# A fused mLSTM attention, token mixer and gated MLP on one core: hand-placed memory, recorded and planned operations, 384-token blocks, no 64-row matmuls

## The chip, the cores and the metric

The kernel runs on one core of one Trainium2 chip. The number is the device time of one execution in microseconds (us); lower is better. TensorE is PE in the profile (its weight loads PEld), VectorE is DVE, ScalarE is ACT, GpSimd is POOL; SP issues the DMAs.

## The reference

Batch 2, 8 heads, 768 tokens, head width 40, model width 320. Three stages follow each other:

```
attention, per batch and head, over tokens t:
  m_new = max(f + m, i);  C = exp(f + m - m_new) C + exp(i - m_new) v k^T;  n likewise with k
  y = sigmoid(o) * (C q) / max(|n q|, 1)
mixer:  u = x + (relu(x^T w_tok1) w_tok2)^T;   x = u + relu(u w_ch1) w_ch2      (256 and 1536 wide)
gMLP:   h = gelu(x w_in); u, v = halves of h (512 each); v = layernorm(v) * g
        x + (u * (w_sg v + b)) w_out
```

The weights come as float64 words, except w_sg.

## The kernel before

**Attention** works in 12 chunks of 128 tokens (6 for each batch). For a chunk, p1 (L322) makes the decay matrix: a matmul psM, 8 exponents on ACT (L336, one for each head, with the row's gate as a bias), a mask on POOL (L338). p2 (L342) makes the scores psS (L350) in full float32 and multiplies them into E on DVE (L351). p3 (L353) makes the chunk's own part psO (L393), the part that comes from the chunks before, psI (L387), which DVE scales (L389) and adds (L396), the new state (psC, L367; DVE L378), the denominators (L400 to L403) and the output `nat` (L406). A float32 matmul shows as two records of the trace.

**Everything behind it** uses a split: each operand is a high part in float32r and a low part, and a product is three matmuls (high by high, low by high, high by low). A weight piece is loaded as float64 words, turned into float32 by one ACT and four DVE instructions (L192 to L198), then split (L170, L171). There are 26 such pieces. The token mixer is tok1 (L430) and tok2 (L473). The channel mixer, ch_phase (L490), runs over blocks of 256 tokens: ch1 makes 128 hidden rows of a block, relu_split (L441) splits them on ACT and DVE, ch2 adds them into two accumulators of 320 columns. The gMLP is part_v (512 columns), and part_u with u, sgu and outp, again over 256 tokens.

Model width 320 is 128 + 128 + 64. For the last 64 rows the high part of the activations stands in partitions 0 to 63 and the low part in 64 to 127 of one tile, so one matmul over 128 rows (L501) makes two of the products, and a second one over the first 64 rows (L502) makes the third. The same pair stands in part_v (L612) and u (L644). These are the 64-row matmuls: 72 + 12 + 24 = 108 in all.

**Order.** Tiles come from pools, and a scheduler orders the instructions by a priority that the author sets by hand in microseconds (`pri(t)`, the tables T_..). Attention of the second batch is interleaved with the channel mixer of the first. Each engine then runs its own list in that order, and waits at an instruction until its inputs are there. All loads are issued by SP in one list.

Of the kernel before, what the change touches and what calls it, by code (L numbers as in the profile page):

```python
# [42 lines left out]
T_AM = [8.0, 13.27, 18.55, 23.82, 29.09, 34.37, 63.39, 71.06, 78.74, 86.41, 94.09, 101.76]
T_AS = [10.69, 13.27, 18.55, 23.82, 27.97, 34.37, 83.43, 71.06, 78.74, 86.41, 92.01, 99.68]
T_AO = [15.0, 17.58, 22.85, 23.54, 27.86, 36.77, 71.33, 79.0, 86.68, 94.35, 99.95, 107.63]
T_AL = [0.5, 0.92, 8.93, 14.2, 19.47, 24.75, 49.62, 57.29, 64.97, 69.12, 74.09, 81.76]
T_T1 = [48.97, 57.14, 64.51, 65.65, 73.01, 80.38, 135.94, 136.48, 137.03, 137.58, 138.13, 138.68]
T_LD = [0.83, 4.35, 7.88, 7.36, 14.94, 18.46, 47.02, 53.09, 59.15, 65.22, 65.06, 71.13, 66.11, 72.67, 79.23, 85.79, 92.35, 167.65, 170.15, 169.68, 174.08, 155.26, 203.02, 224.33, 211.55, 214.86, 196.5, 224.48, 228.45, 251.69, 254.57, 257.07]
T_CV = [8.5, 10.56, 15.55, 19.08, 22.61, 26.13, 55.44, 61.51, 67.58, 67.42, 73.84, 79.56, 82.84, 89.4, 95.96, 102.52, 109.08, 156.7, 165.74, 170.17, 170.47, 181.94, 225.1, 226.29, 227.53, 218.73, 222.99, 224.86, 229.21, 254.43, 278.38, 257.45]
B_CL = [0, 0, 0, 0, 0, 0, 0, 0, 0, 0, 0, 0, 0, 0, 0, 0, 0, 0, 0, 0, 0, 0, 0, 0, 0, 0]  # L50
B_LO = [0, 0, 1, 1, 1, 1, 1, 1, 1, 1, 0, 0, 0, 1, 1, 1, 1, 1, 0, 1, 0, 0, 0, 1, 1, 0, 1, 1, 1, 1, 1, 1]
B_X = [1, 0]
B_V = [1, 1]
B_G = [1, 0]
I32 = mybir.dt.int32
I64 = mybir.dt.int64
# [5 lines left out]

def asf(t):
    return t.bitcast(F32)


@with_exitstack
def tile_mlstm_mixer_gmlp(
# [20 lines left out]
    mm = nc.tensor.matmul  # L89

    def pri(t):
        tc.cur_priority = int(t * 1000)

# [1 line left out]
    base = ctx.enter_context(tc.tile_pool(name="base", bufs=1))  # L95
    ps_m = ctx.enter_context(tc.tile_pool(name="ps_m", bufs=2, space=PSUM))
    ps_acc = ctx.enter_context(tc.tile_pool(name="ps_acc", bufs=2, space=PSUM))

    con = base.tile([128, 131], F32, name="con")
    ident = con[:, 0:128]  # L100
    bdm = con[0:120, 128:131]
    nat = [base.tile([128, NC, DM], F32, name=f"nat{b}") for b in range(B)]
    wst = ctx.enter_context(tc.tile_pool(name="wst", bufs=2))

    def new_uT(pool):
        return [(pool.tile([128, 3, 256], F32R, tag=f"uThi{i}", name=f"uThi{i}"),
                 pool.tile([128, 2, 256], F32R, tag=f"uTlo{i}", name=f"uTlo{i}")) for i in range(3)]

    m1 = ctx.enter_context(tc.tile_pool(name="m1", bufs=1))
    at_cm = tc.tile_pool(name="at", bufs=2, side="right")  # L110
    at = at_cm.__enter__()
    ps_a_cm = tc.tile_pool(name="ps_a", bufs=4, space=PSUM, side="right")
    ps_a = ps_a_cm.__enter__()

# [1 line left out]
    gt_cm = tc.tile_pool(name="gt", bufs=1, side="right")  # L116
    gt = gt_cm.__enter__()
    gates_in = gt.tile([128, 284], F32, name="gates_in")
    fg, ig = gates_in[:, 0:128], gates_in[:, 128:256]
    hm, ind6, ind12 = gates_in[:, 256:264], gates_in[:, 264:270], gates_in[:, 270:282]  # L120
    neg, cap = gates_in[:, 282:283], gates_in[:, 283:284]
    selg = gt.tile([128, 360], F32, name="selg")
    nc.sync.dma_start(out=gates_in, in_=gates_d)
    nc.sync.dma_start(out=con, in_=con_d)

    qT_t, kT_t, kvo_t = {}, {}, {}
    NSET, N3 = 3, 6
    kTm = [at.tile([120, 3, 3, 128], F32, name=f"kTm{i}", bufs=1) if i < 2 else
           m1.tile([120, 3, 3, 128], F32, tag="c2_3", name="kTm2") for i in range(NSET)]
    for t in kTm:  # L130
        nc.gpsimd.memset(t, 0.0)

    def load_chunk(n):
        b, c = divmod(n, NC)
        i = n % NSET if n < N3 else n % 2
        own = i < 2
        qt = (at if own else m1).tile([120, 3, 128], F32, tag=f"qT{i}" if own else "c2_4", name="qT", bufs=1)
        nc.sync.dma_start(out=qt, in_=qT_d[b, c])
        kt = kTm[i]
# [8 lines left out]
    def eng(flag):  # L148
        return nc.gpsimd if flag else nc.vector

    def load_f32(i, pool, tag, src):
        """The float32 values of piece i of the weights; float64 words pass through slot `tag` of `pool`."""
        n = src.shape[1] // (2 if src.dtype == I32 else 1)
        t = wst.tile([128, 768], F32, tag="wt", name="wt", bufs=3)[:, :n]
        pri(T_LD[i])
        if src.dtype == I32:
            raw = pool.tile([128, n, 2], I32, tag=tag, name=f"r_{tag}", bufs=1)
            nc.sync.dma_start(out=raw.rearrange("p n w -> p (n w)"), in_=src)
            pri(T_CV[i])
            to_f32(raw, t, eng(B_CL[i]))  # L160
        else:
            nc.sync.dma_start(out=t, in_=src)
            pri(T_CV[i])
        return t

    def split_piece(i, pool, tag, src):
        """Tile [128, 2, n] in slot `tag` of `pool`: the float32r high parts, then the low parts, of src."""
        t = load_f32(i, pool, tag, src)
        w = pool.tile([128, 2, t.shape[1]], F32R, tag=tag, name=f"w_{tag}", bufs=1)
        nc.scalar.copy(w[:, 0, :], t)  # L170
        eng(B_LO[i]).tensor_tensor(out=w[:, 1, :], in0=t, in1=asf(w[:, 0, :]), op=ALU.subtract)  # L171
        return w
# [28 lines left out]
    def i32(src, a, b):  # L201
        return src[:, a:b].bitcast(I32)
# [491 lines left out]
    for _ in part_v(0):  # L694
        pass
# [110 lines left out]
```

## Time and profile before

| | |
|---|---|
| median of 3 executions | 430.89 us (430.25 to 435.47) |
| the profiled execution: its span, and the only time given of it | 430.5 us |
| PE busy (pipelined matmuls, modelled ends) | 408.4 us, 95% |
| DVE / ACT / POOL busy | 283.7 / 178.4 / 122.8 us |
| matmul records, all instructions | 2629, 7027 |
| bytes moved | 31.14 MB |

Busy time of PE is not work at its peak: a record of a matmul lasts longer than the distance to the next one's start. How long a matmul keeps TensorE is read from the distance of two starts in the timeline. The granted clock stands beside each stretch: 1.00 is the upper of two levels (2.4 GHz), 0.50 the lower (1.2 GHz).

### The profile page before, as it was taken

How to read it: one execution, taken by the hardware profiler on the slowest of the kernel's cores; microseconds unless marked ns; L12 is line 12 of the kernel's file. 1: busy time of each engine (PE TensorE's matmuls, PEld its weight loads, DVE VectorE, ACT ScalarE, POOL GpSimd, SP SyncE). 2: the span in 40 equal slices, each digit the busy share in tenths (PEclk: the TensorE clock that was granted, in tenths of full speed). 3: DMA queues.
4: the chain of work that ended last, by engine and by line, in shares of the span. 5: the costliest groups of instructions: out<-in, count | busy, mean ns of one | idle time of the engine just before them, and what ended most of it. 6: DMA issues, size and time to landing. Idle time of an engine off the chain costs nothing.

```text
span 430.5 us, 7027 instructions
## 1 busy us (share of the span) xinstructions
PE 408.4 (95%) x2629; PEld 365.5 (85%) x2629; DVE 283.7 (66%) x600; ACT 178.4 (41%) x464; POOL 122.8 (29%) x135
## 2 busy tenths in 40 slices
PE   4798898869999999999999999999999999999996
PEld 4697897858899998999888887788878899999996
DVE  5879867997997982279882257445567755455544
ACT  1757455675555521154541153332544522222321
POOL 5537537461223330010110052312626431200000
PEclk9999597996999999999999999999999999999999
DMA  7945354342521000062212030000000000000000
GB/s 225 303 166 205 122 191 158 122 170 87 197 66 49 2 27 12 0 209 63 97 43 69 0 112 0 2 0 2 1 2 2 2 32 0 32 30 17 17 32 32
DMA packets 12239, 31.14 MB, mean 72 GB/s; under 512 B 1644, under 2 KB 6444, under 8 KB 12204
## 3 DMA queue, kind: packets, MB, share of 16 engines
q1 hardware_dynamic: 12204, 30.68, 21.5%
q8 instruction: 21, 0.34, 0.3%
q14 instruction: 14, 0.11, 0.1%
HBM read 28.71 MB, written 1.97 MB: 71 GB/s over the span
## 4 chain that ended last, share of the span: by engine, by line
PE 85%; DVE 8%; issue 2%; ACT 2%; POOL 2%; DMA 1%; POOLq 0%; DVEq 0%; ACTq 0%
PE acc L516 7%; PE ps L502 5%; PE acc L518 5%; PE pss L655 5%; PE acc L517 5%; PE psO L393 4%; PE ps L498 4%; PE pss L657 4%; PE ps L499 4%; PE pss L656 4%; PE ps L500 4%; PE psS L350 3%; PE psu L644 2%; PE psC L367 2%; PE ps L501 2%
## 5 line engine op out<-in xcount | busy, mean ns | idle before, releaser
L442 ACT ACTIVATE a<-ps 128x256 fp32r<-128x256 f32 x72 | 27.8, 386 | 85.4 <-PE ps L502 85.4
L443 DVE SCALAR_TENSOR_TENSOR a<-ps,a 128x256 fp32r<-128x256 f32 x72 | 30.3, 421 | 45.5 <-ACT a L442 45.3
L516 PE MATMUL acc<-w_c,a 128*128 128x320 f32 x144 | 50.8, 354 | 0.2 <-ACT a L442 0.2
L517 PE MATMUL acc<-w_c,a 128*128 128x320 f32 x144 | 44.4, 309 | 0.0
L518 PE MATMUL acc<-w_c,a 128*128 128x320 f32 x144 | 44.3, 310 | 0.0
L498 PE MATMUL ps<-uThi,w_c 128*128 128x256 f32 x144 | 42.6, 296 | 0.0
L655 PE MATMUL pss<-w_c,v 128*128 128x256 f32 x144 | 42.2, 293 | 0.0
L499 PE MATMUL ps<-uTlo,w_c 128*128 128x256 f32 x144 | 41.4, 287 | 0.0
L500 PE MATMUL ps<-uThi,w_c 128*128 128x256 f32 x144 | 41.2, 286 | 0.0
L657 PE MATMUL pss<-w_c,v 128*128 128x256 f32 x144 | 40.5, 281 | 0.0
L656 PE MATMUL pss<-w_c,v 128*128 128x256 f32 x144 | 40.3, 280 | 0.0
L350 PE MATMUL psS<-qT,kTm 120*128 120x128 f32 (+1 forms) x192 | 31.4, 318 | 3.4 <-DVE E L351 2.5
L580 ACT ACTIVATE sq<-psu 128x256 f32<-128x256 f32 x24 | 9.2, 384 | 59.7 <-PE psu L644 59.7
L516 PEld LDWEIGHTS acc<-w_c,a 128*128 128x128 f32 x144 | 26.9, 187 | 8.0 <-issue 0.7
L171 POOL TENSOR_TENSOR w_c<-wt,w_c 128x768 fp32r<-128x768 f32 (+1 forms) x13 | 22.9, 1775 | 35.4 <-ACT w_c L170 35.3
L350 PEld LDWEIGHTS psS<-qT,kTm 120*128 120x128 f32 (+1 forms) x192 | 28.7, 226 | 4.2 <-DVE E L351 2.7
L336 ACT ACTIVATE E<-psM,wT 128x128 f32<-128x128 f32 x96 | 27.5, 380 | 8.7 <-PE psM L332 8.3
L393 PEld LDWEIGHTS psO<-kvo,E 128*128 128x128 f32 x192 | 28.9, 224 | 0.6
L655 PEld LDWEIGHTS pss<-w_c,v 128*128 128x128 f32 x144 | 27.3, 190 | 2.2
L498 PEld LDWEIGHTS ps<-uThi,w_c 128*128 128x128 f32 x144 | 28.0, 194 | 1.0 <-issue 0.7
L338 POOL TENSOR_SCALAR_AFFINE_SELECT E<-E 128x512 f32<-128x512 f32 x24 | 18.5, 772 | 34.1 <-ACT E L336 34.1
L393 PE MATMUL psO<-kvo,E 128*128 128x41 f32 x192 | 28.2, 302 | 0.0
(196 smaller groups left out, 1115.1 us busy)
## 6 DMA issues: line engine op xcount, KB each, us to landing
kvo<-in_kvo_dram SPq DMA_DIRECT2D x12, 504.0 KB
r_c<-in_ch_dram SPq DMA_DIRECT2D x5, 768.0 KB
r_c<-in_ch_dram SPq DMA_DIRECT2D x6, 640.0 KB
wt<-in_wsg_dram SPq DMA_DIRECT2D x6, 384.0 KB
qT<-in_qT_dram SPq DMA_DIRECT2D x12, 180.0 KB
kTm<-in_kT_dram SPq DMA_DIRECT2D x36, 60.0 KB
out_dram<-y SPq DMA_DIRECT2D x12, 160.0 KB
r_wA<-in_tok_dram SPq DMA_DIRECT2D x3, 512.0 KB
```

What stands on the lines that cost most here:

```text
L350: mm(ps[:, j, :], kt[0:r, jj, g, :], qt[0:r, g, :], start=True, stop=True)
L393: mm(psO[:, h, :], E[h // 4][:, h % 4, :], v1[:, h, :], start=True, stop=True)
L443: nc.vector.scalar_tensor_tensor(out=lo, in0=ps, scalar=0.0, in1=asf(hi), op0=ALU.max, op1=ALU.subtract)
L498: mm(ps, c1(0, k, m), hi[:, k, :], start=(k == 0), stop=False)
L499: mm(ps, c1(0, k, m), lo[:, k, :], start=False, stop=False)
L500: mm(ps, c1(1, k, m), hi[:, k, :], start=False, stop=False)
L516: mm(acc[j], ah[:, js], wh, start=(m == m0), stop=False)
L517: mm(acc[j], ah[:, js], wl, start=False, stop=False)
L518: mm(acc[j], al[:, js], wh, start=False, stop=(m == m2 - 1))
L655: mm(ps, v[:, 0, ds_], wsg[s][:, 0, ts], start=(s == 0), stop=False)
L656: mm(ps, v[:, 0, ds_], wsg[s][:, 1, ts], start=False, stop=False)
L657: mm(ps, v[:, 1, ds_], wsg[s][:, 0, ts], start=False, stop=(s == NC - 1))
```

## The change

The whole kernel is recorded and then ordered by a planner; memory is placed by hand. What differs in the computation:

- **No 64-row matmuls.** `transpose_split` copies the last 64 columns twice side by side, so that the transposed tile has the same 64 rows in both halves; the weights' tile has the high part above the low part. Two matmuls over 128 rows (L688, L689) then make all products. Same for v (L815, L816) and u (L841, L842).
- **Blocks of 384 tokens** instead of 256 in ch1, u and sgu. ch2 and the output matmuls keep 320 columns and have three accumulators.
- **Exponents in one pass.** The row's gate is put into the matmul's left operand (LR), so one ACT instruction of 512 columns makes four heads. LR is filled through four small DMAs of gate rows (L441) and ACT copies (L444).
- **Queries scaled.** A small matmul psW (L554, three for a chunk) spreads the decay of the queries; DVE multiplies it into q (L555). Then the part from earlier chunks and the chunk's own part add up in the same PSUM tile (L581, L583), and L389, L396 and the copy L398 fall away.
- Old and new state: ACT scales the old one (L567), DVE or POOL adds (L575). Sigmoid as 1 + tanh, the factor 2 in the denominator.
- **Order.** Every operation is recorded with its tiles' regions. PE keeps the order of the program, but may take a later matmul when the next one's inputs are late by the planner's durations; the other engines go by when the matmul that needs them is due. Low parts of splits go to DVE or POOL as the planner finds them free. In the program the attention of both batches stands ahead of the channel mixer of either: chunk n's p3 stands beside p1 of chunk n + 2, p2 of n + 1, tok1 of n - 1 and, from n = 7, tok2 of the first batch.

The diff, cut:

```diff
-            mm(ps, c1(0, 2, m), hi[:, 2, :], start=False, stop=False)
-            mm(ps, c1(1, 2, m), hi[0:64, 2, :], start=False, stop=True)
+                mm(p, w[:, ms], hi[:, 2, ts], start=False, stop=False)
+                mm(p, w[:, ms], lo[:, 2, ts], start=False, stop=True)
...
-        nc.scalar.copy(hi[:, 0:2, sl], ps[:, 0:2, :])
-        nc.scalar.copy(hi[0:64, 2, sl], ps[0:64, 2, :])
+        tl = tl_s[s % 2]
+        act.copy(tl.rearrange("p (r n) -> p r n", r=2), nat[:, b, s, 256:320].unsqueeze(1).to_broadcast([128, 2, 64]))
+        pe.transpose(p[:, 2, :], tl, ident)
+        act.copy(hi, p)
+        dve.tensor_tensor(out=lo, in0=p, in1=asf(hi), op=ALU.subtract)
...
+    def split_tails(name, col, n, src):
+        t = to_f32(name, col, n, src)
+        a, b = sb(name, col, n, F32R), sb(name, col + n, n, F32R)
+        act.copy(a[lo], t[lo])
+        flex.tensor_tensor(out=a[up], in0=t[lo], in1=asf(a[lo]), op=ALU.subtract)
...
-        NB = 256
+NB = 384
...
-                for j in range(4):
-                    h = 4 * hf + j
-                    nc.scalar.activation(out=E[:, j, :], in_=ps[:, j, :], func=AF.Exp,
-                                         bias=wTv[b][:, 2, h, c:c + 1])
+            mm(p, LR[:, n, :], MR[b][:, 4 * hf:4 * hf + 4, :], start=True, stop=True)
+            act.activation(out=E[:, hf], in_=p.rearrange("p (j t) -> p j t", j=4), func=AF.Exp)
...
-                nc.vector.tensor_tensor(out=t1, in0=psI, op=ALU.mult,
-                                        in1=wTv[b][:, 0, :, c].unsqueeze(2).to_broadcast([128, H, 41]))
+            act.activation(out=qm, in_=asf(wq_t[b]), func=AF.Copy, scale=ind6[:, c:c + 1])
+            for g in range(3):
+                mm(psW[:, g, :], selr[:, 120 * g:120 * g + 120], qm, start=True, stop=True)
+            dve.tensor_tensor(out=qs, in0=psW, in1=qt, op=ALU.mult)
...
+        act.activation(out=dn[:, 1, :], in_=psO[:, :, 40], func=AF.Abs)
+        dve.tensor_scalar(out=dn[:, 0, :], in0=dn[:, 1, :], scalar1=1.0, scalar2=2.0, op0=ALU.max, op1=ALU.mult)
...
+        for o in reversed(ops):
+            tail = 0.0 if o.eng == "PE" else 2.4 + o.nbytes / 3.0e5 if o.eng == "SP" else o.dur
+            for s in o.suc:
+                d = s.due - s.dur - (0.0 if same else o.lat + self.LAT)
+                o.due = min(o.due, d)
+            o.key = o.i if o.eng == "PE" else o.due - tail
...
+    for n in range(N):
+        if n + 2 < N:
+            p1(n + 2)
+        if n + 1 < N:
+            p2(n + 1)
+        p3(n)
+        if n + 3 < N:
+            load_chunk(n + 3)
+        for i in early.get(n, ()):
+            tok_weights(i)
+        for f in late.get(n, ()):
+            f()
+        b, c = divmod(n, NC)
+        if n >= 1:
+            m = n - 1
+            tok1(m // NC, m % NC)
+        if n == NC:
+            tok_hidden()
+        if n > NC:
+            s = n - NC - 1
+            tok2(0, s, X)
+            transpose_split(0, s, X)
...
+    ch_steps(jobs, extra)
+    Z, Q = (2, 3, 4), (0, 1)
+    for i, (b, blk, d) in enumerate(seq):
+        part_sgu(b, blk, d, Q)
...
+    with tc.manual_schedule():
+        plan.issue()
```

What this makes of the engines' lists is shown at three places. First PE in the channel mixer, one step of ch1 (ps) and the ch2 matmuls behind it. Before:

```order
L498 MATMUL ps_2379<-uThi_2102,w_c_00_1084 128x256
L499 MATMUL ps_2379<-uTlo_2103,w_c_00_1084 128x256
L500 MATMUL ps_2379<-uThi_2102,w_c_00_1084 128x256
L498 MATMUL ps_2379<-uThi_2102,w_c_01_1095 128x256
L499 MATMUL ps_2379<-uTlo_2103,w_c_01_1095 128x256
L500 MATMUL ps_2379<-uThi_2102,w_c_01_1095 128x256
L501 MATMUL ps_2379<-uThi_2102,w_c_02_1106 128x256
L502 MATMUL ps_2379<-uThi_2102,w_c_02_1106 128x256
L516 MATMUL acc<-w_c_1_1133,a 128x320
```

And now the same step, with L684 to L689 for L498 to L502 and L699 to L701 for L516 to L518:

```order
L684 MATMUL ps<-uT,c__149 128x384
L685 MATMUL ps<-uT,c__149 128x384
L686 MATMUL ps<-uT,c__149 128x384
L684 MATMUL ps<-uT,c__151 128x384
L685 MATMUL ps<-uT,c__151 128x384
L686 MATMUL ps<-uT,c__151 128x384
L688 MATMUL ps<-uT,c__153 128x384
L689 MATMUL ps<-uT,c__153 128x384
L699 MATMUL ps<-c__156,a 128x320
```

A step has the same eight ch1 matmuls, 384 columns wide, with no 64-row one among them (L502 was it); behind it stand nine ch2 matmuls instead of six, and there are 48 steps instead of 72.

Second PE in the attention of the second batch in the changed kernel, from one chunk's p1 (L528) over p2 (L540), transposes of the first batch (L645, L648), psW (L554), the new state (L563) to psO (L581, L583):

```order
L528 MATMUL ps<-MR,LR 128x512
L540 MATMUL ps<-qT,kTm 128x128 x3
L645 MATMUL ps<-con,nat 128x128 x2
L648 MATMUL ps<-con,tail 128x128
L540 MATMUL ps<-qT,kTm 128x128 x2
L528 MATMUL ps<-MR,LR 128x512
L540 MATMUL ps<-qT,kTm 128x128 x3
L554 MATMUL ps<-qm,selr 120x128 x3
L563 MATMUL ps<-wv,kvo 120x123 x2
L563 MATMUL ps<-wv,kvo 120x82
L630 MATMUL ps<-x,w__137 128x320
L581 MATMUL ps<-nb,qs 128x123 x2
```

Where the kernel before had matmuls of ch1 and ch2 between those of the second batch's chunks, only tok1, tok2 and transposes stand there now; the first ch1 matmul comes behind the last chunk's psO.

Third DVE at the end of the attention in the changed kernel, from the last chunk's output (L588) to the first split weights of ch2 (`c__156`); `rc` and `wt` are weight pieces on their way to float32:

```order
L588 TENSOR_TENSOR nat<-tn,dn 128x320
L368 SCALAR_TENSOR_TENSOR wt<-rc__152,wt 128x768
L652 TENSOR_TENSOR uT<-ps,uT 128x3x128
L387 TENSOR_TENSOR c__153<-wt,c__153 64x768
L652 TENSOR_TENSOR uT<-ps,uT 128x3x128
L636 SCALAR_TENSOR_TENSOR hl<-ps,hh 128x320 x2
L775 TENSOR_SCALAR gln<-gln 128x4
L363 TENSOR_SCALAR wt<-wt 128x640
L364 TENSOR_SCALAR wt<-wt 128x640
L366 SCALAR_TENSOR_TENSOR wt<-rc__155,wt 128x640
L639 TENSOR_TENSOR nat<-ps,nat 128x320
L368 SCALAR_TENSOR_TENSOR wt<-rc__155,wt 128x640
```

The conversion of the first ch2 piece starts only behind the last chunk's output; two relu splits and the piece's low part (L377) follow, and the first ch2 matmul (L699) waits for that.

## Rows read from the trace of the kernel before

**Rows 1.** The page, part 1 and 2: PE's busy time; its clock by slice.

```profile
PE 408.4 (95%) x2629; PEld 365.5 (85%) x2629; DVE 283.7 (66%) x600; ACT 178.4 (41%) x464; POOL 122.8 (29%) x135
...
PEclk9999597996999999999999999999999999999999
```

**Rows 2.** Windows: length, then busy us (instructions) by engine, clock, DMA.

```profile
core 0: us, PE busy (x) PEld busy (x) DVE busy (x) ACT busy (x) POOL busy (x), PEclk, DMA share, GB/s
0.00:104.00 104.00, 85.49 (x497) 78.95 (x498) 82.34 (x156) 56.56 (x162) 54.91 (x58) 0.87 0.52 173
42.00:56.00 14.00, 12.17 (x54) 11.60 (x55) 11.48 (x24) 5.59 (x20) 7.27 (x9) 0.51 0.39 128
104.00:431.00 327.00, 322.88 (x2134) 286.51 (x2132) 201.36 (x445) 121.82 (x304) 67.84 (x77) 1.00 0.12 40
```

**Rows 3.** Timeline of PE: start, duration, line; around a 64-row matmul (L502).

```profile
179.56 0.28 PE L500 MATMUL ps<-uThi,w_c 128*128 128x256 f32 x1
179.68 0.28 PE L501 MATMUL ps<-uThi,w_c 128*128 128x256 f32 x1
179.88 0.38 PE L502 MATMUL ps<-uThi,w_c 64*128 64x256 f32 x1
180.19 0.41 PE L437 MATMUL acc<-x,w_wA 128*128 128x320 f32 x1
180.44 0.31 PE L438 MATMUL acc<-x,w_wA 128*128 128x320 f32 x1
...
180.88 0.31 PE L438 MATMUL acc<-x,w_wA 128*128 128x320 f32 x1
```

**Rows 4.** Groups by line and shape: 64-row matmuls (count, busy, mean).

```profile
L502 PE MATMUL ps<-uThi,w_c 64*128 64x256 f32 x72 | 27.7, 385 | 0.0
...
L644 PE MATMUL psu<-xT,w_wB 64*128 64x256 f32 x12 | 4.6, 381 | 0.0
...
L612 PE MATMUL psv<-w_wA,xT 64*128 64x512 f32 x6 | 3.0, 499 | 0.0
```

**Rows 5.** Timeline of PE: float32 matmuls early, and at full clock.

```profile
24.23 1.77 PE L393 MATMUL psO<-kvo,E 128*128 128x41 f32 x8
...
59.45 0.83 PE L350 MATMUL psS<-qT,kTm 120*128 120x128 f32 x6
60.12 0.98 PE L393 MATMUL psO<-kvo,E 128*128 128x41 f32 x8
60.93 0.36 PE L350 MATMUL psS<-qT,kTm 80*128 80x128 f32 x1
```

**Rows 6.** Groups by line, DVE's and ACT's: count, busy us, mean ns.

```profile
L351 DVE TENSOR_TENSOR E<-psS,E 128x512 f32<-128x512 f32 x24 | 16.4, 683 | 7.6 <-PE psS L350 6.3 <-POOL E L338 1.2
L194 DVE TENSOR_SCALAR wt<-wt 128x512 int32<-128x512 int32 (+3 forms) x26 | 15.8, 610 | 0.1
L193 DVE TENSOR_SCALAR wt<-wt 128x512 f32<-128x512 f32 (+3 forms) x26 | 13.9, 537 | 0.5 <-ACT wt L192 0.4
L378 DVE SCALAR_TENSOR_TENSOR cb<-cb,decT,ct 120x123 f32<-120x123 f32 (+1 forms) x24 | 11.1, 501 | 2.2 <-ACT ct L373 2.0
L196 DVE SCALAR_TENSOR_TENSOR wt<-r_c,wt 128x640 int32<-128x640 int32 (+1 forms) x11 | 10.1, 916 | 0.0
L406 DVE TENSOR_TENSOR nat<-th,dn 128x320 f32<-128x320 f32 x12 | 7.9, 657 | 0.8 <-POOL th L405 0.7
L402 DVE TENSOR_SCALAR dn<-dn 128x8 f32<-128x8 f32 x12 | 5.1, 425 | 0.0
L396 DVE TENSOR_TENSOR t<-psO,t 128x328 f32<-128x328 f32 x10 | 4.9, 491 | 2.9 <-PE psO L393 2.9
...
L336 ACT ACTIVATE E<-psM,wT 128x128 f32<-128x128 f32 x96 | 27.5, 380 | 8.7 <-PE psM L332 8.3
```

**Rows 7.** The line of the chunks' outputs: durations, first and last start.

```profile
L406 DVE TENSOR_TENSOR nat<-th,dn x12: 475/489/1018, 29.6 to 158.2; 128x320 f32<-128x320 f32 x12
```

**Rows 8.** Timeline of PE: the last matmul.

```profile
426.83 0.31 PE L676 MATMUL pso<-w_x,gs 128*128 128x320 f32 x1
```

More of the change, by code (lines that the diff above doesn't have):

```diff
@@ L103, in tile_mlstm_mixer_gmlp @@
[L103 to L113, printed above, removed]
@@ L127, in tile_mlstm_mixer_gmlp @@
-    NSET, N3 = 3, 6
-    kTm = [at.tile([120, 3, 3, 128], F32, name=f"kTm{i}", bufs=1) if i < 2 else
-           m1.tile([120, 3, 3, 128], F32, tag="c2_3", name="kTm2") for i in range(NSET)]
-    for t in kTm:
-        nc.gpsimd.memset(t, 0.0)
+    plan = Plan(nc)
+    for d in (qT_d, kT_d, kvo_d, gates_d, con_d, selg_d, tok1_d, tok2_d, ch1_d, ch2_d, win_d, wsg_d, wout_d,
+              gln_d, bsg_d, out):
+        plan.dram.add(d.tensor.name)
+    pe, act, dve, pool, sp = (Engine(plan, e) for e in ("PE", "ACT", "DVE", "POOL", "SP"))
@@ L133, in load_chunk @@
+    qs_s = [r_tmp.take("qs", 384)[0:120].rearrange("p (g t) -> p g t", g=3) for _ in range(2)]
+    qm_s = [r_x.take("qm", 128, F32R) for _ in range(2)]
+    th_s = [r_tmp.take("th", 320).rearrange("p (h d) -> p h d", h=H) for _ in range(2)]
+    tn = r_tmp.take("tn", 320).rearrange("p (h d) -> p h d", h=H)
+    dn_s = [r_x.take("dn", 16).rearrange("p (r h) -> p r h", r=2) for _ in range(2)]
     def load_chunk(n):
         b, c = divmod(n, NC)
-        i = n % NSET if n < N3 else n % 2
-        own = i < 2
@@ new lines, in tile_mlstm_mixer_gmlp, with tok_hidden, tok2 @@
+    hh, hl = (sb(nm, WK + 6144 + 640 * i, 640, F32R).rearrange("p (m n) -> p m n", m=2)
+              for i, nm in enumerate(("hh", "hl")))
+    def tok_hidden():
+        for m in range(2):
+            relu_split(ps[:, ACC[m], 0:DM], hh[:, m, :], hl[:, m, :])
+    def tok2(b, s, banks):
+        p = bank(banks)[:, 0:DM]
+        for k in range(2):
+            mm(p, w2(0, k, s), hh[:, k, :], start=(k == 0), stop=False)
+            mm(p, w2(1, k, s), hh[:, k, :], start=False, stop=False)
+            mm(p, w2(0, k, s), hl[:, k, :], start=False, stop=(k == 1))
+        residual(p, b, s)
@@ new lines, in tile_mlstm_mixer_gmlp, with tok_b1 @@
+    tok2(0, 5, X)
+    tok1(1, 5)
+    transpose_split(0, 5, X)
+    tok_hidden()
+    Y = (5, 6, 7)
+    def tok_b1(s):
+        tok2(1, s, Y)
+        transpose_split(1, s, Y)
+    extra = {2 * s + 1: [functools.partial(tok_b1, s)] for s in range(NC)}
+    extra[2] = [lambda: ch1_weights(1, 0)]
+    extra[4] = [lambda: ch1_weights(1, 1)]
+    for i in range(3):
+        extra[6 + 2 * i] = [functools.partial(ch2_weights, 3 + i)]
+    jobs = [(0, blk) for blk in range(4)]
+    r_tmp = Region(sb, TMP, TMP + 3264)
```

1182 lines of the change are left out of this document (642 added, 540 removed).

## The prediction

> **What bounds the kernel now.** I read the page's busy table first: PE is busy 95% of the span [rows 1], but pipelined records overlap, so this says only where to look. The clock line under it has its low slices in the first quarter. The windows cut the span there [rows 2]. From 104 us on PE is busy 322.9 of 327 us at a granted clock of 1.00 (2.4 GHz), DVE 201 of 327: nothing but TensorE's own pace counts in that stretch. Up to 104 us PE is busy 85 of 104 us, DVE 82.3 (79%), and the mean clock is 0.87; between 42 and 56 us it is 0.51, the 1.2 GHz level, while PE has 54 records in 14 us. So there are two regimes: a first one in which PE and DVE wait for each other and the clock falls, and a second one, three quarters of the span, where each nanosecond of a matmul's pace is paid.
>
> What a matmul keeps TensorE is the distance between starts, not the duration [rows 3]: 256 columns 0.12 us (179.56 to 179.68), 320 columns 0.147 us (180.44 to 180.88 is three). That is 0.00042 us a column more; 384 columns then cost 0.174 us and 512 0.228 us (estimates along this line). The float32 ones cost 0.112 us a record for the scores (six in 0.67 us) and 0.101 us for psO (eight in 0.81 us); at 24 us the same eight psO records take 1.77 us instead of 0.98 [rows 5], so the first 28 us or so are at the lower level too, whatever the clock column shows there.
>
> **PE's own work, before.** Counted from the loops: 720 matmuls of 320 columns, 105.8 us; 1200 of 256 (the 64-row ones in them), 144.0; 120 of 512, 27.4; scores 192 records, 21.5; psO 192, 19.4; psC and psI 120 at 0.105, 12.6; 72 transposes at 0.11, 7.9; gates 1.5. This is 340.1 us, without what the 64-row matmuls cost on top.
>
> **The 64-row matmuls.** Around L502 [rows 3] the distances are 0.20, 0.31 and 0.25 us where neighbours of their widths have 0.12, 0.12 and 0.147: 0.37 us more, of which most falls on the matmul ahead and the one behind. There are 108 of them [rows 4] (the L644 and L612 groups stand there once for each batch), so 40.3 us, nearly all of it in the stretch where PE never waits. So before: 340 + 40 = 380 us of PE at full clock; the other 50 us of the 430.5 are the head, the end (3.4 us behind the last matmul's end at 427.1, [rows 8]), half clock and waits, nearly all ahead of 104 us. The changed kernel puts 128-row matmuls of the same columns in their place: minus 40.3 us.
>
> The row weighs against a rule of the Trainium skill. "TensorEngine Tiling (Array Packing)", Performance Considerations, says to use row tiles where the contracted side is 64 or less, since two such tiles can run beside each other; by this rule the 64-row matmuls would be the cheap ones, and the removal would give nothing: 40 us more than my sum. The same page, Key Properties, says that changing the tiling mode drains the engine, and that is how the trace's distances look.
>
> **Wider blocks.** 1200 matmuls of 256 columns become 800 of 384: 144.0 to 139.2 us, minus 4.8. Bounds: if 384 columns cost 0.160 us (columns at 2.4 GHz alone) minus 16; if in proportion to the 256 ones (0.18) nothing.
>
> **Queries scaled.** 30 psW matmuls of 128 columns at 0.1 us (no row has one; a transpose with 128 columns has 0.11, the least of the column line is 0.07): plus 3 us, ends 2 and 5. PE's work after: 340.1 - 4.8 + 3 = 338.3 us.
>
> **Attention.** It now stands alone ahead of the mixer. PE's part up to the last psO: scores 21.5, psO 19.4, psC and psI 12.6, psM 24 of 512 columns 5.5, psW 3, gates 1.5, 62 tok1 matmuls 9.1, 24 of tok2 3.5, 12 transposes 1.3: 77.4 us at full clock, which leaves 261 us behind it. When it ends, DVE decides. Its list up to the last output holds, with the durations of [rows 6]: 9 weight pieces at 0.54 + 0.61 + 0.92 + 0.92 (L198 taken like L196), 26.8 with one low part; 24 score products at 0.683, 16.4; 10 outputs, 5 wv and 7 low parts of x at 0.657, 14.5; 12 state adds at 0.50, 6.0; 12 tn and 8 residuals and splits at 0.49, 9.8; 14 with 384 columns from PSUM (qs, uT) at an estimated 0.55, 7.7; 4 spreads, 2.7; some 49 small ones at 0.3 (L402's 0.425 includes a wait for its own engine), 14.7. Sum 98.6 us. With no idle DVE this would end at about 100 us, at the share of before (79%) at 124. I take 115 us, 85%: each chunk is now prepared two chunks ahead, so DVE has more to choose from, but PE is near its limit too: half speed in the first 28 and another 27 us, as before, leaves some 76 of 104 us, and it has 77 to do. The chunks of the first batch before came at 7.8 us each; twelve such from 24 us on end at 118, which agrees.
>
> Several additions I cost at nothing. On ACT, 96 exponents at 0.38 us become 24 of four times the columns, and some 70 small ones come in their place (old state, queries, doubled tails, LR): about even, and ACT has 47 of 104 us idle [rows 2]. If that cover went, the denominators would be late: L585 on DVE waits for ACT's L584, and behind it on DVE queue the output and the next score product. POOL loses its 12 products of the output and gets low parts, with 49 of 104 us idle. The four DMAs for LR stand on SP's list between the first chunks' loads; they delay kvo and weight loads by their issue, while the scores need only the loads ahead of them. A chunk's loads wait for the p3 three chunks ahead, and on SP's list the ch1 and ch2 weights queue behind them; these are needed only at 115 us.
>
> **Waits behind it.** Each ch step has 2.7 us of PE against 0.5 for ACT and 0.5 for DVE, with two steps of slack, so I count none there. Three places have thin cover. At the start the first ch2 weights come about 10.5 us of DVE work behind the last output, against 10 us of PE work: 3 us. At the change to the gMLP the last v goes through ACT, DVE and POOL while PE has some 7 us of other work: 2 us. At the end the last product with w_sg is followed by four instructions, 2.3 us, covered by one group of nine matmuls, 1.3 us: 2 us with semaphores. Together 7, ends 3 and 13.
>
> **Sum.** 115 + 261 + 7 + 3.4 = 386 us, against 430.5 of the profiled execution, whose span lies 0.4 us under the median. In steps: -40.3 - 4.8 + 3 = -42 us of PE work, -2 of head, half clock and waits together.
>
> **Rivals.**
> 1. Attention at the lower clock throughout. PE's 77 us become 155, so it ends near 157 us, and 157 + 261 + 7 + 3 = 428. For it: while 1.2 GHz is granted PE is the slowest engine, and nothing of ch1 is there any more to fill it. Against it: in 42 to 56 us before PE was still busy 12 of 14 us, and the level rose again. The Trainium skill ("TensorE: Matmul & The Clock Gate", Part 1) has the lower level as the default that activity lifts; the row from 42 to 56 us agrees in that the lower level stands in the part in which PE has waits [rows 2]. 7 in 100.
> 2. The price of the 64-row matmuls does not come back, because neighbours that change shape (120 and 80 rows of the scores) or the wider ones pay it too: 386 + 40 = 426. Against it: the score of 80 rows that starts at 60.93 us follows psO's 128 rows with no more than their own distance [rows 5]. This is also the skill's packing rule. 3 in 100.
> 3. Slower: in each chunk PE at 1.2 GHz (12.9 us) and DVE's two score products (1.4) follow each other instead of overlapping, because the fixed order has each wait for the other: 14.3 us a chunk, 172 us for twelve, 172 + 272 = 444. It is slower than before from an attention end beyond 168 us. Against it: before, the chunks' outputs came 11.7 us apart on average, from 29.6 to 158.2 us [rows 7], with ch1 and ch2 of the mixer between them. 2 in 100.
> 4. DVE without gaps: attention ends at 100, no wait behind it: 100 + 261 + 3 + 3 = 367. This lies in my range.
>
> **Range and chances.** Forecast with its bounds (attention end 100 to 130, 384 columns 0.160 to 0.18, waits 3 to 13): 364 to 410, 86 in 100; below it 2. 2% of the median is 8.6 us, about what these runs can tell apart. Faster than 422.3 us: forecast, the part below and a third of rival 1, 0.90; within 2%: the rest of 1, and 2, 0.08; slower 0.02.
>
> **What would show it.** In the changed trace: a distance of about 0.174 us between matmuls of 384 columns and none of 0.2 or 0.3 around L688 and L689 (step right); the last L588 at 100 to 130 us; behind it PE busy without gaps at 1.00. Wrong: clock 0.5 over most of the attention, or idle PE ahead of L699 in many steps.

## The result and the profile after

The changed kernel takes 373.9 us (median of 4 runs, 373.3 to 376.0), the kernel before 431.9 us beside it (4 runs, 430.3 to 435.5): a ratio of 0.865, 95% interval 0.859 to 0.871. The forecast of 386 us has the right direction and is 12 us too long. The profiled execution took 376.0 us, the slowest of the four; its span is 374.3.

The page of the changed kernel, busy table, PE's slices and the granted clock in tenths, answers to [rows 1]:

```profile
PE 356.9 (95%) x2257; PEld 344.5 (92%) x2257; DVE 264.7 (71%) x519; ACT 175.8 (47%) x384; POOL 76.2 (20%) x96
PE   4799999999979999998999999999999999999995
PEclk9999999999999999999899999999999999999999
```

The share of PE is 95% as before, and still the profiled span is 56 us shorter: the share told nothing. What changed is what a busy PE does in a microsecond. The clock line now has one slice below 9.

The windows of the changed kernel answer to [rows 2] (busy us and count of each engine, granted clock, DMA share, GB/s):

```profile
0.00:104.00 104.00, 95.38 (x695) 89.93 (x695) 80.30 (x176) 66.74 (x169) 40.39 (x54) 1.00 0.70 227
42.00:56.00 14.00, 13.40 (x108) 12.59 (x107) 11.35 (x27) 10.11 (x27) 6.61 (x10) 1.00 1.02 343
104.00:374.00 270.00, 261.51 (x1564) 254.55 (x1562) 184.38 (x344) 109.03 (x216) 35.83 (x42) 0.99 0.08 28
28.00:104.00 76.00, 75.00 (x607) 72.51 (x605) 65.62 (x141) 51.15 (x133) 31.10 (x38) 1.00 0.65 212
```

Between 42 and 56 us PE had 54 records at 0.51 before; now it has 108 at 1.00. From 28 to 104 us PE is busy 75.0 of 76 us, DVE 65.6. DVE is busy 80.3 us up to 104 us. The prediction's 98.6 us are a sum of durations, and DVE's records overlap a little at their ends; counted in the same way, by durations up to 103.6 us, its list is 88.6 us.

PE's timeline of the changed kernel around L688 and L689 (start, us, engine, line, operation), which answers to [rows 3]:

```profile
151.25 0.33 PE L684 MATMUL ps<-uT,c__151 128*128 128x384 f32 x1
151.42 0.33 PE L685 MATMUL ps<-uT,c__151 128*128 128x384 f32 x1
151.60 0.33 PE L686 MATMUL ps<-uT,c__151 128*128 128x384 f32 x1
151.77 0.33 PE L688 MATMUL ps<-uT,c__153 128*128 128x384 f32 x1
151.94 0.33 PE L689 MATMUL ps<-uT,c__153 128*128 128x384 f32 x1
152.12 0.31 PE L701 MATMUL ps<-c__156,a 128*128 128x320 f32 x1
```

Five steps lead from 151.25 to 152.12 us, 0.174 us each, and the two tails (L688, L689) stand no farther apart than the others. The estimate was 0.174.

The last product of the output (L588) answers to [rows 7]; 12 of them, 10 on DVE and 2 on POOL:

```profile
L588 DVE TENSOR_TENSOR nat<-tn,dn x10: 481/492/750, 28.2 to 103.1; 128x320 f32<-128x320 f32 x10
```

The attention ends at 103.6 us, not 115. PE's longest waits in the changed kernel (line, releaser, us in total, times, longest), without those for the gates, the keys and the first exponents:

```profile
PE ps L699 <- ACT wo L376: 2.0, 1, 2.0
PE ps L528 <- ACT LR L444: 1.4, 1, 1.4
PE ps L645 <- DVE nat L639: 1.2, 2, 0.9
PE ps L630 <- ACT x L626: 0.7, 1, 0.7
PE ps L684 <- DVE a L636: 0.5, 1, 0.5
PE ps L867 <- ACT gs L857: 0.5, 1, 0.5
PE ps L631 <- POOL x L627: 0.4, 1, 0.4
```

L528's lies at 10.8 us, a first one of 0.3 us at L645 at 96 us, the others behind 104. The one of 2.0 us stands at 176.5 us, where the prediction had no wait at all.

### The profile page after: what moved, and what is told of

Read it like the earlier page. It is cut to its first block, busy times and chain, and to the rows that moved or that the text cites. A ratio compares the mean times of both kernels' runs of the same rounds, so it can differ in the third digit from the quotient of the medians.

```text
span 374.3 us, 5950 instructions
## 1 busy us (share of the span) xinstructions
PE 356.9 (95%) x2257; PEld 344.5 (92%) x2257; DVE 264.7 (71%) x519; ACT 175.8 (47%) x384; POOL 76.2 (20%) x96
## 3 DMA queue, kind: packets, MB, share of 16 engines
q1 hardware_dynamic: 12428, 30.79, 25.1%
## 4 chain that ended last, share of the span: by engine, by line
PE 87%; DVE 5%; ACT 3%; DMA 2%; POOL 1%; issue 1%; SPq 0%; DVEq 0%; ACTq 0%; POOLq 0%
PE ps L699 6%; PE ps L701 6%; PE ps L700 6%; PE ps L540 6%; PE ps L853 5%; PE ps L684 4%; PE ps L852 4%; PE ps L851 4%; PE ps L686 4%; PE ps L685 4%; PE ps L583 4%; PE ps L689 2%; PE ps L688 2%; DMA kTm<-in_kT_dram 2%; PE ps L867 2%; PE ps L868 2%
## 5 line engine op out<-in xcount | busy, mean ns | idle before, releaser
L635 ACT ACTIVATE a<-ps 128x384 fp32r<-128x384 f32 x48 | 23.5, 491 | 44.3 <-PE ps L689 44.2
L636 DVE SCALAR_TENSOR_TENSOR a<-ps,a 128x384 fp32r<-128x384 f32 x48 | 26.5, 554 | 19.7 <-ACT a L635 19.5
L853 PE MATMUL ps<-wsg,v 128*128 128x384 f32 x96 | 32.4, 337 | 0.0
L851 PE MATMUL ps<-wsg,v 128*128 128x384 f32 x96 | 32.3, 337 | 0.0
L852 PE MATMUL ps<-wsg,v 128*128 128x384 f32 x96 | 32.3, 337 | 0.0
L540 PE MATMUL ps<-qT,kTm 120*128 120x128 f32 (+1 forms) x192 | 29.3, 302 | 0.7 <-DMA kTm<-in_kT_dram 0.7
L540 PEld LDWEIGHTS ps<-qT,kTm 120*128 120x128 f32 (+1 forms) x192 | 27.9, 214 | 2.1 <-issue 0.9
L639 DVE TENSOR_TENSOR nat<-ps,nat 128x320 f32<-128x320 f32 x48 | 21.9, 487 | 9.3 <-PE ps L701 5.9
L799 DVE SCALAR_TENSOR_TENSOR sq<-sq,ps 128x384 f32<-128x384 f32 (+1 forms) x28 | 16.9, 608 | 9.5 <-ACT sq L798 9.3
L583 PE MATMUL ps<-kvo,E 128*128 128x41 f32 x192 | 23.0, 280 | 0.0
L583 PEld LDWEIGHTS ps<-kvo,E 128*128 128x128 f32 x192 | 22.5, 193 | 0.0
L853 PEld LDWEIGHTS ps<-wsg,v 128*128 128x128 f32 x96 | 18.0, 188 | 0.3 <-DVE v L826 0.3
L851 PEld LDWEIGHTS ps<-wsg,v 128*128 128x128 f32 x96 | 18.0, 188 | 0.1
L852 PEld LDWEIGHTS ps<-wsg,v 128*128 128x128 f32 x96 | 18.0, 188 | 0.0
```

The costliest lines, as they stand in the source:

```text
L540: mm(p[:, j, :], kt[0:r, jj, g, :], qt[0:r, g, :], start=True, stop=True)
L583: mm(psO[:, h, :], E[:, h // 4, h % 4, :], v1[:, h, :], start=(c == 0 and h == 0), stop=(h == H - 1))
L635: act.activation(out=hi, in_=p, func=AF.Relu)
L636: dve.scalar_tensor_tensor(out=lo, in0=p, scalar=0.0, in1=asf(hi), op0=ALU.max, op1=ALU.subtract)
L639: dve.tensor_tensor(out=nat[:, b, s], in0=p, in1=nat[:, b, s], op=ALU.add)
L851: mm(p, v[:, 0, ds_], wsg[s][:, 0, ts], start=(s == 0), stop=False)
```

## The experiments

Three questions were open: is it the 64-row matmuls that gave the 40 us, and what about them; what sets the attention's end; and what is the stall at 176.5 us. The medians that follow stand against 373.9 us for the changed kernel and 430.8 to 431.1 us for the kernel before. The kernel before ran beside each of them, the changed kernel did not, so a difference of one or two microseconds from 373.9 says little.

**1. The kernel before without its 64-row matmuls.**

```diff
+            nc.gpsimd.tensor_tensor(out=w[64:128, 1, :], in0=t[own], in1=t[own], op=ALU.subtract)
-        r = 64 if k == 2 and p else 128
-        return c1t[m // 6, k][0:r, p, ...]
+        return c1t[m // 6, k][:, p, ...]
...
-            mm(ps, c1(1, 2, m), hi[0:64, 2, :], start=False, stop=True)
+            mm(ps, c1(1, 2, m), hi[:, 2, :], start=False, stop=True)
```

(and the same in L612 and L644; the added line fills the other 64 rows with zeros.)

> The kernel before, with nothing changed but its 108 matmuls on 64 rows: the low weights' tile gets 64 rows of zeros and these matmuls run on 128 rows, with the same columns and the same sums. Theory (a 64-row matmul among 128-row ones costs 0.37 us, wherever it stands): 431 - 40 = 391 us, 386 to 397; the distances around L502 fall to 0.12 us. Rival A (the gain of the changed kernel is order and wider blocks; 64-row matmuls are cheap): 425 to 433 us. Rival B (the price is real but half of it lies in waits that stay): 405 to 415 us.

Measured: 395.5 us, 4 runs, from 386.9 to 397.7; the profiled one took 397.3, its mean clock 0.944. That is 33 to 44 us less than before: rivals A and B fall. PE's timeline of this run at the place of L502, which answers to [rows 3]:

```profile
185.76 0.28 PE L501 MATMUL ps<-uThi,w_c 128*128 128x256 f32 x1
185.88 0.28 PE L502 MATMUL ps<-uThi,w_c 128*128 128x256 f32 x1
186.00 0.31 PE L516 MATMUL acc<-w_c,a 128*128 128x320 f32 x1
```

The distances are 0.12 us, as the theory asked. The median misses the 40 by 5 us and the fastest run exceeds them by 4; three of the four runs lie 7 to 11 us above the fastest, so how much of the price comes back here is not known more closely. The clock of the first 104 us is no better than before (0.75 from 28 to 56 us, 0.76 before), so the upper level that the changed kernel has there isn't this edit's.

**2. The changed kernel with 64-row matmuls put back**, one of each pair, then both, then one on 96 rows (the lines of these three kernels stand one further: L690 is L689 of the change).

```diff
-                mm(p, w[:, ms], lo[:, 2, ts], start=False, stop=True)
+                mm(p, w[0:64, ms], lo[0:64, 2, ts], start=False, stop=True)
```

> The changed kernel with the second tail matmul of L689, L816 and L842 put back on 64 rows (76 matmuls; the products of two low parts are left out, which before had not either). Theory: 76 x 0.37 = +28, 402 us, 397 to 406, with PE still without gaps behind the attention. Rival A (64 rows cost nothing by themselves, only next to narrow columns): 374 to 378. Rival C (the price is a share of the columns' time, so 384 columns pay more than 256): above 410.

> As the run before, but both tail matmuls (L688 and L689, L815 and L816, L841 and L842) on 64 rows; the products with the low parts of the tail weights are left out. If the price is paid at the two changes of the row count, a pair of neighbours on 64 rows pays it once: about as the run with one of them, +28, 399 to 406 us. If each 64-row matmul pays for itself: +56, 424 to 432 us. If only the part on the 64-row matmul itself (0.19 of the 0.37 us) is paid by each: +42, 414 to 418 us.

> The changed kernel with the second tail matmul on 96 rows (part of the products of two low parts left out). Theory (the price belongs to the 64-row setting, not to fewer than 128 rows; the scores of 80 rows showed none): 372 to 376 us, no change. Rival (any change of the row count pays): 399 to 406 us.

Measured: 402.5 us (402.3 to 402.9) with one, 401.8 (401.1 to 404.3) with both, 375.2 (373.0 to 375.8) on 96 rows. One costs 28.6 us, 0.376 us for each of 76 (64 at 384 columns, 12 at 512), the same as the 0.37 read at 256. Both cost no more than one, and 96 rows nothing that can be measured (the distances there stay at 0.17 us), so the rivals of the first and the last and the other two outcomes of the second fall. PE's timeline with one, then with both:

```profile
151.28 0.34 PE L687 MATMUL ps<-uT,c__151 128*128 128x384 f32 x1
151.46 0.33 PE L689 MATMUL ps<-uT,c__153 128*128 128x384 f32 x1
151.72 0.44 PE L690 MATMUL ps<-uT,c__153 64*128 64x384 f32 x1
152.09 0.44 PE L686 MATMUL ps<-uT,c__151 128*128 128x384 f32 x1
152.37 0.34 PE L687 MATMUL ps<-uT,c__151 128*128 128x384 f32 x1
```

```profile
151.08 0.34 PE L687 MATMUL ps<-uT,c__151 128*128 128x384 f32 x1
151.35 0.44 PE L689 MATMUL ps<-uT,c__153 64*128 64x384 f32 x1
151.63 0.34 PE L690 MATMUL ps<-uT,c__153 64*128 64x384 f32 x1
151.89 0.44 PE L686 MATMUL ps<-uT,c__151 128*128 128x384 f32 x1
152.17 0.34 PE L687 MATMUL ps<-uT,c__151 128*128 128x384 f32 x1
```

Against 0.174 us, the distances with one are 0.26, 0.37, 0.28: 0.09 + 0.20 + 0.11. With both they are 0.27, 0.28, 0.26, 0.28, about 0.1 more each. So a change between 128 and 64 rows costs some 0.2 us, half on the matmul ahead of it and half on the one behind, and a matmul between two changes carries a half of each. The price belongs to the change, not to the matmul. At 512 columns the same run has 0.32, 0.43 and 0.27 us around a 64-row matmul (234.51 to 235.53 us), against 0.23, 0.23 and 0.17 without one. The Trainium skill's page "TensorEngine Tiling (Array Packing)", Key Properties, says that a change of the tiling mode drains the engine; these runs agree in that time is lost at the change, 0.2 us here, but what TensorE does in that time they do not show. What the same page says of speed with 64 rows needs two tiles at work beside each other, which no run here shows.

**3. 256-token blocks in the changed kernel.**

```diff
-NB = 384
+NB = 256
...
-    jobs = [(0, blk) for blk in range(4)]
+    jobs = [(0, blk) for blk in range(6)]
```

(and the loops over a block's chunks and the steps of the other work to match.)

> The changed kernel with 256-token blocks in the channel mixer and in the gMLP's u and gate products: 1200 matmuls of 256 columns in place of 800 of 384, half as many instructions more on ACT and DVE there; everything else as it was. Theory (PE alone sets that stretch): 1200 x 0.12 - 800 x 0.174 = +4.8 us, 377 to 382. Rival A (the price is the columns alone): 373 to 375. Rival B (the fixed parts of ACT's and DVE's instructions come onto the path): 386 to 400.

Measured: 385.0 us (382.0 to 386.3), +11.1: above the theory's 377 to 382 and mostly short of rival B's 386 to 400; rival A falls. The distances at 256 columns are 0.12 us, which is the +4.8 expected; the trace shows waits that the changed kernel has not:

```profile
PE ps L699 <- DMA rwsg<-in_wsg_dram: 3.1, 1, 3.1
PE ps L666 <- DVE hl L636: 2.7, 1, 2.7
PE ps L688 <- DVE c__153 L387: 1.9, 1, 1.9
```

These are 7.7 us. With the smaller ones PE's waits behind the gates, the keys and the first exponents come to 8.8 us, against 5.5 for the same sum in the changed kernel, and the clock falls to 0.91 from 104 to 140 us. A run with other instructions also has another planned order; how much of the 6 us is the narrower blocks' own stays open.

**4. What sets the attention's end: more work for DVE, or for PE.** Both are put in where the operations are issued, so the planned order of everything else is that of the changed kernel.

```diff
         for o in self.order():
             at_line(o.line)(getattr(self.real[o.eng], o.name), o.a, o.k)
+            for _ in range(2 if o.line == 541 else 0):
+                self.real["DVE"].memset(self.scr, 0.0)
...
```

```diff
         for o in self.order():
+            for _ in range(3 if o.line == 528 else 1):
                 at_line(o.line)(getattr(self.real[o.eng], o.name), o.a, o.k)
```

> The changed kernel with two memsets of 128 columns behind each of DVE's 24 score products, 48 in all, some 0.17 to 0.25 us each: 8 to 12 us more on DVE up to 103 us, where it has 20 us idle. Theory (PE sets the pace of the attention, not DVE): 374 to 378 us. Rival, which is the step of the prediction (DVE decides when the attention ends): 382 to 386.

> The changed kernel with each of the 24 psM matmuls (L528, 512 columns) issued three times: 48 more at 0.23 us, 11 us of PE work up to 95 us, the result the same. Theory (PE sets the pace of the attention): 374 + 9 to 13 = 383 to 387 us. Rival (DVE decides, as the prediction had it): 374 to 378.

Measured: 376.7 us (375.7 to 377.2) with DVE's extra work, 384.1 (383.2 to 386.8) with PE's. The run with more for DVE: its memsets, and the line of the outputs:

```profile
L268 DVE MEMSET scr<- 128x128 f32 x48 | 7.9, 165 | 2.2
L588 DVE TENSOR_TENSOR nat<-tn,dn x10: 481/493/782, 27.9 to 104.4; 128x320 f32<-128x320 f32 x10
```

The run with more for PE, the window from 28 to 104 us and the same line:

```profile
28.00:104.00 76.00, 75.58 (x593) 72.88 (x593) 59.67 (x129) 48.47 (x125) 26.54 (x35) 1.00 0.55 179
L588 DVE TENSOR_TENSOR nat<-tn,dn x10: 482/492/898, 29.9 to 112.1; 128x320 f32<-128x320 f32 x10
```

7.9 us more on DVE put the last output off by 1.3 us (104.4 against 103.1) and the median by 2.8; 11 us more on PE put it off by 9.0 and the median by 10.2. PE sets the pace, though DVE is not free either. The two tests are not of one size: part of the memsets falls under the ends of their neighbours, and DVE's busy time up to 104 us grows by 4.3 us only (80.3 to 84.6). With more for PE, PE stays busy for 75.6 of the 76 us; DVE, which waits for it, falls from 65.6 to 59.7.

**5. The exponents in four instructions of 128 columns.**

```diff
-            act.activation(out=E[:, hf], in_=p.rearrange("p (j t) -> p j t", j=4), func=AF.Exp)
+            for j in range(4):
+                act.activation(out=E[:, hf, j], in_=p[:, 128 * j:128 * j + 128], func=AF.Exp)
```

> The changed kernel with the exponents of a half in four instructions of 128 columns, 96 in place of 24. ACT gets some 20 us more work, all of it in the first 95 us, where it is busy about three quarters. Theory (DVE and PE set that stretch, ACT has room): 374 to 380 us. Rival (ACT is nearly full there, and the exponents lie in each chunk's chain): 385 to 395 us.

Measured: 371.7 us (370.6 to 372.3), 2 us less. The cost was expected too high, and the sign was wrong; the rival falls. In the first 104 us ACT's rows read, changed kernel first:

```profile
L529 ACT ACTIVATE E<-ps 128x512 f32<-128x512 f32 x24 | 14.3, 596 | 4.8 <-PE ps L528 4.6
```

```profile
L530 ACT ACTIVATE E<-ps 128x128 f32<-128x128 f32 x96 | 19.4, 281 | 8.6 <-PE ps L528 8.2
```

Four in a row take 5 us more in all, not 20. With other instructions the planner gives another order; in it the last output starts at 98.4 us, 5 us sooner. So no gain from "one pass" is shown: this run has lost it and is no slower. What it costs in one and the same order was not tried. An order that the planner finds is good to a few microseconds only.

**6. No planned order: the operations issued as recorded.**

```diff
-        for o in self.order():
+        for o in self.ops:
```

> The changed kernel with its operations issued in the order in which they are recorded, not in the planned one; the 46 or so low parts and products that the planner gave to POOL fall back to DVE. Theory (the planned order is what lets DVE fill 88% of the stretch up to 103 us and keeps PE so busy that its clock stays up): the attention ends at 120 to 140 us, part of it again at the lower clock, and the run takes 393 to 415 us. Rival (the engines wait for the same data in either order): 374 to 380 us.

Measured: 623.0 us (620.6 to 625.3). The theory's direction is right, its size is off by 200 us. The page's clock line and PE's longest group of waits:

```profile
PEclk9985555655656585675789999999989788989999
```

```profile
PE ps L630 <- ACT x L626: 86.8, 11, 17.7
```

In recorded order the mixer's first matmul (L630) stands on PE's list ahead of the next chunk's work, and PE waits 11 times for ACT's copy of a finished chunk (L626), 8 us each. In the stretch with these waits the granted clock is near the lower level (0.53 from 60 to 180 us), and the last output starts at 297.9 us. So the changed kernel needs an order made for it: as recorded it is 192 us slower than the kernel before. The row edit alone does not need it (experiment 1). What a planned order is worth by itself in the kernel before was not tried.

**7. The stall at 176.5 us.** The trace names ACT's conversion of w_out (L376) as what PE waited for. But L699 reads no w_out. The program's waits for this matmul name a DMA queue too:

```
745 L699 MATMUL ps_58<-c2__158,a_117 128x320 [waits DMAHW0_49,Activation_49]
```

That queue's count is reached by a load of w_sg issued at 175.14 us (its first piece, 384 KB; one load of w_sg stands ahead of it, at 144.8 us). Its buffer shares 256 of its columns with the first columns of the w_ch2 piece that L699 reads. The planner compares exact ranges and sees no conflict, since L699 reads other columns; the layer below it makes the matmul wait for the load. So the record of that load alone was put behind the last reader; all engines' lists stay word for word the same.

```diff
-        for o in self.order():
+        od = self.order()
+        w = [o for o in od if o.eng == "SP" and o.k["out"].tensor.name.startswith("rwsg")][1]
+        last = max(j for j, o in enumerate(od) if o.eng == "PE" and self.base.get(o.a[-1].tensor.name) == 14336)
+        od.insert(last, od.pop(od.index(w)))
+        for o in od:
```

> The changed kernel with every engine's list as it was; only the record of the first load of w_sg is put in behind the last matmul that reads the second w_ch2 piece, whose place in memory its buffer overlaps in part. In the changed kernel the matmul L699 at 178.56 us waits for this load (among its semaphores is one of a DMA queue); PE stands for 2.0 us, and then runs 13 matmuls at the lower clock, 1.7 us more. Theory (the wait is for the load): no stall there, 374 - 3.7 = 370.3 us, 369 to 371.5. Rival (the wait is for ACT's conversion of w_out, which the trace names): 373 to 375 us, the stall unchanged.

Measured: 374.5 us (373.5 to 375.5, 6 runs): no gain, so the theory's time is missed. PE's timeline at the place, changed kernel first:

```profile
176.19 0.34 PE L689 MATMUL ps<-uT,c__153 128*128 128x384 f32 x1
178.56 0.39 PE L699 MATMUL ps<-c__158,a 128*128 128x320 f32 x1 [2.03 <-ACT wo L376]
178.78 0.44 PE L700 MATMUL ps<-c__158,a 128*128 128x320 f32 x1
179.02 0.47 PE L701 MATMUL ps<-c__158,a 128*128 128x320 f32 x1
```

```profile
176.01 0.33 PE L689 MATMUL ps<-uT,c__153 128*128 128x384 f32 x1
176.19 0.31 PE L699 MATMUL ps<-c__158,a 128*128 128x320 f32 x1
```

The stall is gone, and with it the lower level behind it (distances of 0.27 us for 320 columns, until 182 us). So it was the load, and the releaser named by the trace was wrong: here L699 starts at 176.19 us, ahead of ACT's conversion (L376) at 177.90. In the run with more for DVE, whose lists are the changed kernel's too, the trace itself puts the same wait of 2.0 us down to the load (rwsg). But the chain of waits of the run with the late load shows where the time went (start, us, what):

```profile
177.69 4.55 DMA rwsg<-in_wsg_dram
...
182.32 0.07 ACT wsg L396
...
183.06 0.48 ACT a L635
...
183.93 0.72 ACT wsg L396
```

ACT's list has the conversion of that load (L396) ahead of the next half of the hidden layer (L635). The load now starts 2.5 us later and lands at 182.24, ACT stands until then, and PE waits 1.6 us at L684 and 0.6 at L699 behind it. The wait moved from PE to ACT, and from there back to PE.

**8. Both ends of that load moved.** On the kernel with four exponents (which had 2.3 us of the same wait), the load's record is moved as above, and the planner takes such a load to land 2.5 us later, so that the conversions come later in ACT's and DVE's lists:

```diff
-                o.end = queue + 0.6
+                o.end = queue + (3.1 if o.nbytes == 393216 else 0.6)
```

> The kernel with the exponents in four instructions (371.7 us), with two edits against its wait for w_sg (2.3 us at L700): the record of the first w_sg load stands behind the last matmul that reads the second w_ch2 piece, and the planner takes loads of 393,216 bytes to land 2.5 us later than it did, so that ACT's and DVE's conversions of w_sg come later in their lists. Theory (the wait moved in the run with the late load alone because ACT's list had the conversion ahead of the next half's outputs): no wait for w_sg on PE, ACT or DVE; 371.7 - 2.3 - 0 to 1.5 = 368 to 369.5 us. Rival (whatever is moved, the 2 MB of w_sg come when ACT and DVE have no room): 371 to 373 us.

Measured: 369.9 us (367.2 to 370.0, 6 runs), a ratio of 0.858 to before, interval 0.856 to 0.861: 4 us below the changed kernel. The median lies just above the theory's 368 to 369.5 and below the rival's 371. PE has no wait for w_sg any more; apart from those for the gates and the first keys the longest is of 0.8 us. ACT still waits 2.1 us for one of these loads, which the theory had excluded; no wait of PE for that conversion follows.

**9. The lower level in the first 25 us.** Eleven matmuls of zeros fill PE's waits in the first 12 us.

```diff
+        fill, (p, x) = {448: 8, 540: 1, 528: 2}, self.fil
+        self.real["DVE"].memset(asf(x), 0.0)
         for o in self.order():
+            for _ in range(fill.pop(o.line, 0)):
+                self.real["PE"].matmul(p, x[:, 0:128], x, start=True, stop=True)
...
```

> The changed kernel with 11 matmuls of zeros (512 columns) put on PE where it waits in the first 12 us: 8 ahead of L448, 1 ahead of the first L540, 2 ahead of the first L528; every other list as it was. In the changed kernel PE has 10.5 us of waits up to 20 us and runs at the lower level until 25.2 us. Theory (the level rises earlier where PE has no waits): PE's 13 us of work between 12 and 25 us shrink by up to 6 us, of which the first chunks' chains over ACT and DVE take part back: 369 to 372.5 us. Rival A (the level rises at 25 us anyway): 373 to 375. Rival B (the zeros delay the gates): 375 to 378.

Measured: 374.2 us (372.2 to 374.9, 6 runs): no change that can be measured. PE's timeline of this run:

```profile
7.42 1.38 PE L540 MATMUL ps<-qT,kTm 120*128 120x128 f32 x10 [0.61 <-DMA kTm<-in_kT_dram]
...
13.46 0.77 PE L528 MATMUL ps<-MR,LR 128*128 128x512 f32 x1
...
20.65 2.45 PE L540 MATMUL ps<-qT,kTm 120*128 120x128 f32 x16
```

Ten score records take 1.38 us at 7.4 us, which is the upper level; at 13.5 us L528 takes 0.77 us, the lower one, and from about 22 us on it is up for good, 3 us sooner than in the changed kernel (there 16 score records from 21.60 on take 3.72 us). The last output starts at 100.8 us in place of 103.1. So the level did rise after the zeros, but PE waited again, for the keys, for LR and for the first exponents, and it fell. Rival A's range holds the time, but its reason fails, since the level is up sooner. What was won at the attention's end is within the spread of the six runs; whether some of it reaches the end stays open.

## Why the prediction was right, and where it was not

- **64-row matmuls, -40.3: right.** 76 of them put back cost 28.6 us, 0.376 each; 108 make 40.6. In the kernel before alone the edit gave 33 to 44. That the neighbours would go on paying (rival 2) is refuted by the distances around L688. One reading was off: not most of the 0.37 us falls on the matmul ahead and the one behind, but half, 0.08 and 0.10; the 64-row matmul itself has 0.19.
- **Wider blocks, -4.8: the size of the matmuls was right**, 0.174 us as estimated. Undone, the blocks cost 11.1 us, of which the distances give 4.8; whether the rest is theirs is open (experiment 3).
- **The attention's end, 115 us: this step failed.** The prediction said "When it ends, DVE decides", and took a list of 98.6 us at a share of 85%. The list was 10 us too long: the 22 products of the output, wv and the low parts of x took 11.3 us against 14.5, the weight pieces 24.2 against 26.8 (nine at its four prices are 26.9 already, without the low part), the state adds 4.6 against 6.0, the small instructions some 12 against 14.7. The 88.6 us that the list lasts are 85.5% of 103.6 us, so with the right list the step would have given the measured end. That would have been luck: the 79% that the share came from is busy time, not a sum of durations, and experiment 4 shows that it is PE that decides. By the prediction's own prices PE has done some 8 of its 77.4 us when the level rises at 25.1 us; 25.1 + 69.4 is 94.5, and the last psO ends at 99.6, the last output at 103.6. Of the 5 us between, 0.9 are waits; the rest are distances wider than priced (in the mean 0.109 us for a record of psO, priced at 0.101, and 0.29 for psM, priced at 0.228).
- **"Half speed in the first 28 and another 27 us, as before": half of this failed.** The first stretch came (until 25.1 us), the second did not; PE is busy 13.4 of 14 us in it now. It was this stretch that had made PE look nearly out of time. Rival 4 has the nearer time (367 us) with the wrong engine.
- **Costed at nothing.** ACT's additions: right, and even 96 exponents in place of 24 cost 5 us of ACT and, in another planned order, nothing at the end. The four loads of LR: PE waits 1.4 us for them at 10.8 us, while DVE and ACT are at the gates. In the run of experiment 7 the same wait of 1.4 us is put down to DVE's spread (L476), so without the loads it would most likely have stood too.
- **Waits behind the attention, 7 us: the size was right by luck, the places were not.** At the start of the channel mixer 2.5 us stand against 3, but for tok1's input (L630, L631), a transpose (L645) and a relu split (L684); the first ch2 matmul, for whose weights the 3 us were put down, has no wait. At the end 0.5 stand against 2, at the change to the gMLP none against 2. In their place came the wait for w_sg, 2.0 us and 1.6 more of the lower level behind it (9 matmuls of 320 columns 0.11 longer, 4 of 384 columns 0.15): 6.6 in all. The prediction looked at late data; this matmul waited for a load that it does not read.
- **The order** had no price in the sum, only a share of DVE that it would allow. Experiment 6 shows what hangs on it: in recorded order the same operations take 623 us.
- **The range** of 364 to 410 us is narrower than its bounds taken together, which give 356 to 412; the measured time lies within either.

With the attention's end as it was, the prediction's sum is 103.6 + 261 + 7 + 3.4 = 375.0 us; the profiled span is 374.3. Of the 56 us between the two spans some 41 are the 64-row matmuls (experiment 2) and 5 the widths. Which of the other changes gave the rest, some 11 us, is open: order, placement, scaled queries and exponents changed together, and of these only the exponents were put back by themselves in a kernel with a planned order.

## What to carry to other kernels

Price a matmul by the distance to its neighbours, and look for changes of its row setting among them: here each costs two halves of 0.1 us that the busy share does not show, and 64 rows of zeros are cheaper than a matmul on 64 rows. Before saying which engine ends a stage, add up every engine's list at the clock that it will have there, take list and share by the same measure, and test it by giving each engine more to do. Where a stall's named releaser makes no data for the waiting instruction, look at its semaphores and at buffers that share memory; and move both ends of a late load, its start and its reader, or the wait only changes engines.

## What was not expected of the hardware

- The 0.2 us of a change between 64 and 128 rows is the same at 256, 320, 384 and 512 columns, and is paid once for a run of 64-row matmuls; 96 rows among 128 cost nothing (375.2 us against 373.9).
- A single wait of 2.0 us at 176.5 us, after 150 us at the upper level, was followed by the lower one until 182 us, though PE had no wait in between; in the run with the wait moved, waits of 1.6 and 0.6 us that end 2.3 us apart were not (granted clock 1.00 from 176 to 200 us, against 0.93 in the changed kernel). In recorded order the granted clock was 0.53 from 60 to 180 us, a stretch full of waits. The page's clock line shows 9 for the first 25 us, while L528 takes 0.77 us there and 0.48 us from 26.9 us on; here the durations, not the column, fit the distances between the matmuls.
- The load of w_sg's first piece, 384 KB, took 4.55 us from issue (177.69 us) to landing in the run of experiment 7, where three others of its size had been issued 1.2 to 2.2 us ahead of it.
